# A fused attention and highway kernel: one query load in two pieces, the last stores in pairs, and a new order of work

## The chip, the cores and the metric

The kernel runs on one core of a Trainium2 chip. A core has five engines that work side by side, each with its own queue: TensorE (PE in the profile, with its weight loads as PEld), VectorE (DVE), ScalarE (ACT), GpSimd (POOL) and SyncE (SP), which computes nothing and issues transfers. Transfers (DMAs) that SyncE or ScalarE issue run on the core's DMA engines. The metric is the device time of one execution in microseconds (us), lower is better.

## What is computed

Eight batches of eight heads, 576 positions, 64 values each: an attention without the usual score matrix, then a highway layer on the 4608 x 512 result.

```python
def _attn_ref(q, k, v):
    q_s = softmax of q over its last axis
    k_s = softmax of k over the positions
    kv = np.einsum('bhsd,bhse->bhde', k_s, v)
    return np.einsum('bhsd,bhde->bhse', q_s, kv)

def _moe_ref(x, w_h, w_t, b_t):
    H = np.maximum(x @ w_h, 0.0)
    T = 1.0 / (1.0 + np.exp(-(x @ w_t + b_t)))
    return T * H + (1.0 - T) * x
```

The first function is shortened here: in the reference each softmax is written out. Between the two, x is the attention's output with the heads side by side, one row of 512 for each position.

## The kernel before

Each batch gives four and a half tiles of 128 rows; two batches share the ninth, so tile 8, 17, 26 and 35 hold rows of two batches, and 36 tiles come from four pairs of batches (`tiles`, from L129). A position is p * 9 + j, with p in 64 partitions for each of two heads and j from 0 to 8.

All work is a list of steps, `ORDER` (L16 to L64), and `tc.manual_schedule()` (L465) emits them in this order. Each engine executes its own steps in the order of the list; between engines the framework puts in the waits that the data and the buffers need. It also gives each DMA one of a few semaphores that tells of its landing. A suffix names an engine where there is a choice: A for ScalarE, D for VectorE, P for GpSimd.

For each batch b:

- `k_b_c`, `q_b_j`, `v_b_c` load (L187, L192), in SyncE's queue. `ld` has 3 buffers for each of k and v, `ldq` 4 for q. k and v of batches 0 and 1 come in two halves (c = 0 and 2). `Q_CUTS` (L176) is empty, so `q_b_0` is the whole query of a batch; `load_q` (L190) already knows a second piece.
- `ek` and `eq` (L244, L291): the exponentials on ScalarE. `vc` (L250) casts v, on GpSimd if no suffix says otherwise.
- `kv` (L263): 72 small matmuls, or 36 for one half; `kr` and `kn` (L275, L281) normalize into `kvb` on VectorE.
- `qt` and `qc` (L304, L313): eq transposed on TensorE, and the result moved out of PSUM.

For each tile i:

- `xu` (L331, TensorE), `rs` and `x` (L340, L346, VectorE): attention output, normalized, in 16 bits. Tiles 0 and 4 are done in two halves.
- `xt` (L353, TensorE) and `xe` (L360, ScalarE or VectorE): x transposed.
- `bw` (L372): the bias into a gate bank of PSUM, by a copy on ScalarE (`:A`) or a matmul. `mt` (L384) and `mh` (L393): four matmuls each for gate and carry.
- `th` (L406, L408): tanh on ScalarE. `dd` (L412) on VectorE. `uu` (L425): (tanh + 1) * d on VectorE. `oo` (L442): u + x on GpSimd.
- Where `uu_i_0` has the suffix P, the tile is called lifted: th goes to SBUF, and GpSimd does `ee` (d + x), `uu` (tanh * d) and `oo`. Before, tiles 4, 9, 22 and 26 are lifted.
- `st_i_h_r` (L451, L453, L455): the store. Neighbouring tiles share a buffer of `op` (7 buffers, tag o32) and are stored as a pair in two halves of the partitions, 256 KB each; the steps bear the number of the second tile. Tiles without a mate take a buffer of `o1p` (5 buffers) each. `mate` (L430) gives None for the ninth tiles and for i >= LAST - 4, so tiles 31 to 34 are stored singly, each in two DMAs of 128 KB (L453).
- Tile 35 is split in three by columns (`columns`, L144): 256, 128 and 128 wide, with a gate bank, `th`, `uu`, `oo` and `st` for each. Its first two stores are ScalarE's.

`fill_n_...` (L172): n matmuls of zeros, which keep TensorE at work where it has nothing else to do.

Of the kernel before, what the change touches and what calls it, by code (L numbers as in the profile page):

```python
# [16 lines left out]
b_0 b_32 setuppool fill_16_turned setupdve v_0_0 q_0_0 k_0_0 k_0_2 v_0_2 w_h_0 bsplit w_h_2 vc_0_1:A w_t_0 vc_0_0:D  # L17
fill_4_turned bp bc w_t_2 eq_0_0 v_1_2 eq_0_1 fill_14_xu_0_0 qt_0_0 k_1_2 qc_0_0 ek_0_1 ek_0_0 ek_0_2 k_1_0
fill_7_xu_0_0 kv_0_0 ek_0_3 kr_0_0 kn_0_0 vc_0_2:A vc_0_3 q_1_0 fill_5_xu_0_0 xu_0_0 eq_0_2 rs_0_0 fill_1_xu_0_1
kv_0_1 x_0_0 bw_0 whc_0 qt_0_1 kr_0_1 half qc_0_1:A kn_0_1 v_1_0 whd_1 fill_3_xu_0_1 xu_0_1 whc_2 bw_1 xu_1_0 xt_0_0  # L20
rs_0_1 whd_0 xe_0_0 rs_1_0 x_0_1 v_2_0 wtc_0 fill_2_mh_0_0 mh_0_0 x_1_0 xt_0_1 whd_3 fill_1_qt_1_0 xu_2_0 whd_2 mt_0_0
xe_0_1:D rs_2_0 wtc_2:D xt_1_0 mh_0_1 xe_1_0 x_2_0 mt_0_1 mt_1_0 dd_0 k_2_0 th_0_0 xt_2_0 uu_0_0 xu_3_0 th_1_0 mh_1_0
rs_3_0 xe_2_0 x_3_0 bw_2:A mh_2_0 dd_1 ek_1_3 mt_2_0 ek_1_2 vc_1_3 oo_0_0 vc_1_2 q_2_0 uu_1_0 dd_2 xt_3_0 bw_3 th_2_0
kv_1_1 xe_3_0:D ek_1_1 uu_2_0 mt_3_0 ek_1_0 kr_1_1 kn_1_1 mh_3_0 th_3_0 k_3_0 eq_1_0 dd_3 oo_1_0 oo_2_0 fill_4_qt_1_0
qt_1_0 uu_3_0 vc_1_0:A vc_1_1 bw_4 qc_1_0 eq_1_1 oo_3_0 fill_1_xu_4_0 kv_1_0 v_3_0 kr_1_0 fill_1_xu_4_0 qt_1_1 kn_1_0
qc_1_1:A fill_1_xu_4_0 xu_5_0 xu_4_0 rs_5_0 vc_2_2 rs_4_0 x_5_0 bw_5:A fill_2_xu_4_1 qt_0_2 eq_1_2 x_4_0 fill_1_xu_4_1
xt_5_0 qc_0_2:A xu_6_0 q_3_0 vc_2_0:A xu_4_1 qt_1_2 ek_2_2 k_4_0 v_4_0 q_4_0 xe_5_0:D rs_4_1 rs_6_0 mh_5_0 x_6_0
xt_4_0 qc_1_2 mt_5_0 x_4_1 xe_4_0:D dd_5 xt_4_1 xu_7_0 th_5_0 mt_4_0 xe_4_1:D rs_7_0 ek_2_0 xt_6_0 mh_4_0 mt_4_1
mh_4_1 k_5_0 uu_5_0 x_7_0 xe_6_0:D kv_2_0 dd_4 mh_6_0 kr_2_0 kn_2_0 xt_7_0 dd_6 xe_7_0:D oo_5_0 bw_7:A th_4_0 eq_2_0
uu_4_0:P bw_6:A eq_2_1 qt_2_0 ee_4 xu_8_0 mt_6_0 ek_3_0 rs_8_0 oo_4_0 x_8_0 mt_7_0 th_6_0 qc_2_0 ek_3_2 xt_8_0 uu_6_0  # L30
xu_9_0 mh_7_0 rs_9_0 oo_6_0 eq_2_2 x_9_0 xe_8_0 qt_2_1 dd_7 th_7_0 xu_10_0 xt_9_0 bw_8:A mh_8_0 rs_10_0 vc_3_2 uu_7_0
vc_3_0:A x_10_0 mt_8_0 oo_7_0 dd_8 xe_9_0 kv_3_0 qc_2_1 th_8_0 bw_9:A xt_10_0 uu_8_0 qt_2_2 mh_9_0 eq_3_0 kr_3_0
xe_10_0:D st_5_0_1 oo_8_0 kn_3_0 mt_9_0 bw_10:A v_5_0 eq_3_1 dd_9 xu_11_0 mh_10_0 rs_11_0 ee_9 th_9_0 x_11_0 mt_10_0
eq_3_2 qc_2_2 dd_10 bw_11:A xt_11_0 xu_12_0 th_10_0 uu_9_0:P xe_11_0:D qt_3_0 q_5_0 ek_4_0 rs_12_0 mh_11_0 oo_9_0
x_12_0 uu_10_0 qc_3_0:A xt_12_0 mt_11_0 xe_12_0:D oo_10_0 dd_11 bw_12:A xu_13_0 th_11_0 qt_3_1 rs_13_0 st_1_0_0 vc_4_2
mt_12_0 x_13_0 qc_3_1:A st_1_0_1 uu_11_0 xt_13_0 xu_14_0 ek_4_2 k_6_0 mh_12_0 oo_11_0 rs_14_0 xe_13_0:D x_14_0 mh_13_0
th_12_0 dd_12 bw_13:A xt_14_0 xu_15_0 vc_4_0 uu_12_0 xe_14_0 mt_13_0 eq_4_1 rs_15_0 v_6_0 x_15_0 mh_14_0 dd_13 th_13_0
kv_4_0 bw_14:A oo_12_0 uu_13_0 eq_4_2 qt_3_2 eq_4_0 xt_15_0 kr_4_0 mt_14_0 qc_3_2 kn_4_0 xe_15_0 st_3_0_1 bw_15 dd_14
xu_16_0 th_14_0 mt_15_0 st_3_0_0 rs_16_0 ek_5_2 x_16_0 qt_4_0 uu_14_0 xu_17_0 qc_4_0:A xt_16_0 mh_15_0 rs_17_0 q_6_0
x_17_0 th_15_0 qt_4_1 xe_16_0:D bw_16:A dd_15 xu_18_0 qc_4_1:A xt_17_0 mh_16_0 rs_18_0 xe_17_0:D x_18_0 ek_5_0 mh_17_0  # L40
uu_15_0 st_7_0_1 xu_19_0 eq_5_0 dd_16 st_5_0_0 mt_16_0 rs_19_0 q_7_0 x_19_0 eq_5_2 xt_18_0 qt_5_0 th_16_0 dd_17
bw_17:A oo_13_0 oo_14_0 vc_5_2 vc_5_0 kv_5_0 uu_16_0 qc_5_0:A mt_17_0 kr_5_0 xe_18_0:D bw_18:A kn_5_0 xt_19_0 mh_18_0
th_17_0 v_7_0 xe_19_0:D ek_6_2 uu_17_0 xu_20_0 mt_18_0 rs_20_0 dd_18 bw_19:A qt_5_2 x_20_0 mh_19_0 oo_15_0 oo_16_0
oo_17_0 th_18_0 eq_5_1 uu_18_0 xt_20_0 xu_21_0 st_7_0_0 mt_19_0 oo_18_0 rs_21_0 xe_20_0 bw_20:A th_19_0 vc_6_0 ek_6_0
qc_5_2 x_21_0 qt_5_1 dd_19 xu_22_0 xt_21_0 mh_20_0 rs_22_0 uu_19_0 x_22_0 mt_20_0 bw_21:A xe_21_0:D dd_20 xu_23_0
th_20_0 mh_21_0 rs_23_0 oo_19_0 vc_6_2 qc_5_1:A uu_20_0 xt_22_0 st_19_0_1 mt_21_0 x_23_0 xe_22_0 oo_20_0 k_7_0 dd_21
qt_4_2 st_14_0_0 xu_24_0 th_21_0 mh_22_0 rs_24_0 st_10_0_0 qc_4_2 bw_22:A uu_21_0 eq_6_0 xt_23_0 st_8_0_0 mt_22_0
x_24_0 oo_21_0 dd_22 bw_23:A kv_6_0 th_22_0 xe_23_0:D st_10_0_1 ee_22 eq_7_0 qt_6_0 kr_6_0 mh_23_0 kn_6_0 uu_22_0:P
eq_6_1 xt_24_0 qc_6_0 xu_25_0 mt_23_0 bw_24:A rs_25_0 x_25_0 eq_6_2 st_21_0_1 qt_7_0 xe_24_0 dd_23 xu_26_0 th_23_0
st_21_0_0 xt_25_0 vc_7_2:A mh_24_0 rs_26_0 st_17_0_0 uu_23_0 x_26_0 mt_24_0 xe_25_0 dd_24 bw_25:A xu_27_0 th_24_0  # L50
# [17 lines left out]
def kernel(  # L68
# [11 lines left out]
    B, H, S, D = q.shape  # L80
    DM = H * D
    P = 128
# [38 lines left out]
    T = {}  # L121
# [378 lines left out]
```

## Time and profile before

| | |
|---|---|
| time, median of 3 runs | 124.64 us (124.41 to 125.02) |
| profiled run | 124.86 us, span 122.9 us |
| granted TensorE clock, mean | 0.986 |
| read and written | 30.41 MB and 9.44 MB |

The span runs from the first to the last instruction of the profiled execution. Row 2 of the profile's page cuts it into 40 slices of 3.07 us; each digit is the busy share of a slice in tenths (9 is 90% or more), and the last row has the transfer rate.

```profile
PE   5999999999999999999999999999999999999200
DVE  5802899977989999989999999999999999998510
ACT  4279456887899999999999999899999687774200
POOL 5000102845328684988538547969739564464500
DMA  3999999999999999999999999999989305988842
```

The loads fill the DMA engines up to about 89 us; what follows is stores. A group of instructions in the profile is named by its line, engine and operands, `SPq` is SyncE's queue of DMA issues, and "<-" in a wait stands before what ended it.

### The profile page before, as it was taken

To read this page: it belongs to the slowest core of one execution; us is meant where nothing else is said; L and a number is where in the kernel's file an instruction comes from. 1 tells how busy PE (TensorE), PEld (TensorE's weight loads), DVE (VectorE), ACT (ScalarE), POOL (GpSimd) and SP (SyncE) were. 2 spreads that over 40 slices of the span, in tenths; PEclk is the share of its full clock that TensorE was granted. 3 is DMA by queue.
4 is the path that set the end of the run, shared out by engine and by line. 5 is a ranking of instruction groups with operands and counts; after the bars stand their busy time and mean duration, and the time that the engine had idled before them with its cause. 6 is when DMAs were issued, how large, how long until landed. Compare 5 with 4: busy or idle time off the path is not lost.

```text
span 122.9 us, 3478 instructions
## 1 busy us (share of the span) xinstructions
PE 112.5 (92%) x1392; PEld 65.7 (53%) x1392; DVE 100.9 (82%) x239; ACT 96.3 (78%) x150; POOL 63.9 (52%) x66
## 2 busy tenths in 40 slices
PE   5999999999999999999999999999999999999200
PEld 4645545445556665665566656566665655655100
DVE  5802899977989999989999999999999999998510
ACT  4279456887899999999999999899999687774200
POOL 5000102845328684988538547969739564464500
PEclk9999999999999999999999999999999999999995
DMA  3999999999999999999999999999989305988842
GB/s 119 382 403 402 412 387 391 392 395 381 389 392 388 392 389 388 392 386 402 392 401 396 395 400 403 393 400 395 402 275 249 76 0 108 237 277 264 203 113 87
DMA packets 17077, 40.08 MB, mean 326 GB/s; under 512 B 1187, under 2 KB 1571, under 8 KB 17061
## 3 DMA queue, kind: packets, MB, share of 16 engines
q1 hardware_dynamic: 16768, 39.65, 90.8%
q8 instruction: 11, 0.18, 0.6%
q10 hardware_dynamic: 292, 0.20, 0.5%
q14 instruction: 6, 0.04, 0.1%
HBM read 30.41 MB, written 9.44 MB: 324 GB/s over the span
## 4 chain that ended last, share of the span: by engine, by line
PE 61%; DMA 23%; SPq 3%; ACT 3%; POOL 2%; issue 2%; DVE 1%; DVEq 0%; POOLq 0%
PE tps L384 20%; PE gps L393 20%; DMA v<-in_v_dram 11%; DMA w32h<-in_moe_w_h_dram 8%; PE qps L304 6%; PE xu L331 6%; PE turned L353 6%; PE kv L263 4%; DMA out_dram<-o 3%; POOL o L442 2%; SPq L187 2%; SPq L453 1%; ACT eq L313 1%; ACT qe L291 1%; DVE u L425 1%
## 5 line engine op out<-in xcount | busy, mean ns | idle before, releaser
L442 POOL TENSOR_TENSOR o<-u,x 128x512 f32<-128x512 f16 (+1 forms) x32 | 36.2, 1132 | 30.4 <-DVE u L425 27.2
L384 PE MATMUL tps<-w16t,xT 128*128 128x512 f16 (+2 forms) x152 | 37.1, 368 | 0.0
L393 PE MATMUL gps<-w16h,xT 128*128 128x512 f16 x144 | 36.9, 379 | 0.1
L346 DVE TENSOR_TENSOR x<-xu,rs 128x512 f16<-128x512 f32 (+1 forms) x38 | 24.8, 657 | 0.5
L425 DVE SCALAR_TENSOR_TENSOR u<-tps,d 128x512 f16<-128x512 f32 (+2 forms) x34 | 22.3, 658 | 3.2 <-ACT tps L408 1.4
L412 DVE SCALAR_TENSOR_TENSOR d<-x,gps 128x512 f16<-128x512 f16 x36 | 24.2, 673 | 0.8 <-PE gps L393 0.7
L250 POOL CAST v<-v 128x1152 f16<-128x1152 f32 (+1 forms) x13 | 12.9, 996 | 19.5 <-DMA v<-in_v_dram 19.5
L408 ACT ACTIVATE tps<-tps 128x512 f32<-128x512 f32 (+2 forms) x34 | 18.8, 560 | 4.3 <-PE tps L384 4.0
L291 ACT ACTIVATE qe<-q 128x1024 f16<-128x1024 f32 (+1 forms) x24 | 19.7, 839 | 0.8 <-DMA q<-in_q_dram 0.8
L393 PEld LDWEIGHTS <-xT 128*128 128x128 f16 x144 | 12.8, 98 | 12.4 <-ACT xT L360 0.9
L384 PEld LDWEIGHTS <-xT 128*128 128x128 f16 x152 | 13.4, 98 | 11.2 <-issue 0.2
L244 ACT ACTIVATE ek<-k 128x1152 f16<-128x1152 f32 (+1 forms) x20 | 18.9, 968 | 0.5 <-DMA k<-in_k_dram 0.5
L374 ACT COPY tps<-ball 128x512 f32<-128x512 f32 (+1 forms) x31 | 18.0, 584 | 0.8 <-DVE u L425 0.8
L360 ACT COPY xT<-turned 128x512 f16<-128x512 f16 (+1 forms) x19 | 10.9, 574 | 4.7 <-PE turned L353 4.6
L331 PE MATMUL xu<-kvb,eq 128*128 128x130 f16 (+1 forms) x160 | 14.5, 224 | 0.1
L353 PE MATMUL turned<-idh,x 128*128 128x128 f16 x144 | 14.3, 220 | 0.0
L353 PEld LDWEIGHTS <-x 128*128 128x128 f16 x144 | 10.4, 98 | 6.9 <-DVE x L346 2.7
L304 PE MATMUL qps<-idh,qe 128*128 128x128 f16 x144 | 12.0, 219 | 0.2
L331 PEld LDWEIGHTS <-eq 128*128 128x128 f16 (+1 forms) x160 | 9.9, 100 | 3.7 <-DVE kvb L281 0.8
L304 PEld LDWEIGHTS <-qe 128*128 128x128 f16 x144 | 9.5, 98 | 4.1 <-ACT qe L291 0.8
L313 DVE COPY eq<-qps 128x1024 f16<-128x1024 f16 (+1 forms) x15 | 7.3, 488 | 4.1 <-PE qps L304 4.0
L313 ACT COPY eq<-qps 128x1024 f16<-128x1024 f16 (+1 forms) x9 | 8.5, 940 | 2.5 <-PE qps L304 2.5
(49 smaller groups left out, 98.9 us busy)
## 6 DMA issues: line engine op xcount, KB each, us to landing
q<-in_q_dram SPq DMA_DIRECT2D x8, 1152.0 KB, 13.7
out_dram<-o SPq DMA_DIRECT2D x31, 256.0 KB, 6.2
v<-in_v_dram SPq DMA_DIRECT2D x6, 1152.0 KB, 15.4
k<-in_k_dram SPq DMA_DIRECT2D x6, 1152.0 KB, 15.5
v<-in_v_dram SPq DMA_DIRECT2D x4, 576.0 KB, 10.8
k<-in_k_dram SPq DMA_DIRECT2D x4, 576.0 KB, 10.3
w32h<-in_moe_w_h_dram SPq DMA_DIRECT2D x2, 512.0 KB, 9.8
w32t<-in_moe_w_t_dram SPq DMA_DIRECT2D x2, 512.0 KB, 11.4
```

Source lines behind the costliest of these rows:

```text
L244: nc.scalar.activation(t[:, :, c:c + n].rearrange("p j c d -> p c j d"), T[f"k32{b}"][:, c:c + n].rearrange("p c (j d) -> p c j d", j=NJ), ...
L291: nc.scalar.activation(t[:, j0:j1].rearrange("p j c d -> p c j d"), T[f"q32{b}"].rearrange("p c (j d) -> p c j d", j=NJ)[:, :, j0:j1], AF.Exp)
L304: nc.tensor.matmul(t[:, (j - j0) % 2, 2 * kk:2 * kk + 2, (j - j0) // 2], T[f"qe{b}"][:, j, 2 * kk:2 * kk + 2].rearrange("p c d -> p (c d)" ...
L331: nc.tensor.matmul(dst, T[f"eq{b}_{jp // 2}"][:, jp % 2, n], kvb[b % NKV][:, hh, kk], start=True, stop=True, skip_group_check=True)
L346: nc.vector.tensor_mul(t[:, k0:k1], sums(i, k)[:, :, :, 0:64], T[f"rs{i}_{k}"][:, 0:k1 - k0].unsqueeze(3).to_broadcast([P, k1 - k0, 4, D]))
L353: nc.tensor.matmul(t[:, n], T[f"x{i}"][:, dims(n)], idh, is_transpose=True, start=True, stop=True, skip_group_check=True)
L384: nc.tensor.matmul(gate_bank(i, k if i == LAST else 0), T[f"xT{i}"][:, n], w16["t"][:, n, cs], start=False, stop=(n == 3), skip_group_chec ...
L393: nc.tensor.matmul(t, T[f"xT{i}"][:, n], w16["h"][:, n], start=(n == 0), stop=(n == 3), skip_group_check=True)
L408: nc.scalar.activation(src, src, AF.Tanh, scale=0.5)
L412: nc.vector.scalar_tensor_tensor(t, T[f"x{i}"], -0.5, T[f"gps{i}"], op0=ALU.mult, op1=ALU.max)
L425: nc.vector.scalar_tensor_tensor(t[:, 0:cs.stop - cs.start], gate_bank(i, h), 1.0, T[f"d{i}"][:, cs], op0=ALU.add, op1=ALU.mult)
L442: eng.tensor_add(t[:, 0:w], T[f"u{i}_{h}"][:, 0:w], T[f"{'e' if lifted(i) else 'x'}{i}"][:, cs])
```

## The change

Three edits of the code, and a new list.

```diff
-    Q_CUTS = {}
+    Q_CUTS = {1: 4}
...
     def mate(i):
-        return None if i % 9 == 8 or i >= LAST - 4 else i + 1 if i % 9 % 2 == 0 else i - 1
+        return None if i % 9 == 8 else i + 1 if i % 9 % 2 == 0 else i - 1
...
         if mate(i) is not None:
             eng.dma_start(dst[:, 2 * (jp + r) - 2:2 * (jp + r)], T[f"oo{i - 1}"][rows])
-        elif len(bs) == 1:
-            eng.dma_start(dst[:, 4 * (jp // 2) + 2 * r + jp % 2], T[f"o{i}_{h}"][rows])
         else:
```

The query of batch 1 comes in two pieces, `q_1_0` with positions j = 0 to 3 and `q_1_4` with the rest. Tiles 31 and 32, and 33 and 34, become pairs: `st_31` and `st_33` are gone, `st_32` and `st_34` store both tiles, and their outputs lie in `op` instead of `o1p`.

The list is written anew; it has 706 steps instead of 707. Its beginning up to the second batch's first tiles, before:

```
b_0 b_32 setuppool fill_16_turned setupdve v_0_0 q_0_0 k_0_0 k_0_2 v_0_2 w_h_0 bsplit w_h_2 vc_0_1:A w_t_0 vc_0_0:D
fill_4_turned bp bc w_t_2 eq_0_0 v_1_2 eq_0_1 fill_14_xu_0_0 qt_0_0 k_1_2 qc_0_0 ek_0_1 ek_0_0 ek_0_2 k_1_0
fill_7_xu_0_0 kv_0_0 ek_0_3 kr_0_0 kn_0_0 vc_0_2:A vc_0_3 q_1_0 fill_5_xu_0_0 xu_0_0 eq_0_2 rs_0_0 fill_1_xu_0_1
...
kv_1_1 xe_3_0:D ek_1_1 uu_2_0 mt_3_0 ek_1_0 kr_1_1 kn_1_1 mh_3_0 th_3_0 k_3_0 eq_1_0 dd_3 oo_1_0 oo_2_0 fill_4_qt_1_0
qt_1_0 uu_3_0 vc_1_0:A vc_1_1 bw_4 qc_1_0 eq_1_1 oo_3_0 fill_1_xu_4_0 kv_1_0 v_3_0 kr_1_0 fill_1_xu_4_0 qt_1_1 kn_1_0
qc_1_1:A fill_1_xu_4_0 xu_5_0 xu_4_0 rs_5_0 vc_2_2 rs_4_0 x_5_0 bw_5:A fill_2_xu_4_1 qt_0_2 eq_1_2 x_4_0 fill_1_xu_4_1
xt_5_0 qc_0_2:A xu_6_0 q_3_0 vc_2_0:A xu_4_1 qt_1_2 ek_2_2 k_4_0 v_4_0 q_4_0 xe_5_0:D rs_4_1 rs_6_0 mh_5_0 x_6_0
```

and after:

```
b_0 b_32 setuppool fill_16_turned setupdve v_0_2 k_0_2 q_0_0 k_0_0 v_0_0 w_h_0 bsplit w_h_2 vc_0_3 w_t_0 fill_4_turned
bp ek_0_2 w_t_2 vc_0_2:A ek_0_3 v_1_2 bc fill_8_xu_0_1 kv_0_1 kr_0_1 kn_0_1 eq_0_0 k_1_2 fill_10_xu_0_1 qt_0_0 k_1_0
qc_0_0 fill_4_xu_0_1 xu_0_1 rs_0_1 half vc_0_1 vc_0_0:D q_1_0 x_0_1 whc_0 v_1_0 q_1_4 k_2_0 v_2_0 q_2_0 bw_1:A ek_0_1
eq_0_1 eq_0_2 ek_0_0 bw_0:A fill_6_xu_0_0 kv_0_0 qt_0_1 kr_0_0 xt_0_1 whd_0 kn_0_0 xe_0_1 qc_0_1:A whc_2 fill_3_xu_0_0
xu_0_0 xu_1_0 rs_0_0 rs_1_0 x_0_0 x_1_0 wtc_0 fill_3_mh_0_0 xt_0_0 xe_0_0:D fill_2_mh_0_0 xt_1_0 whd_1 xu_2_0 whd_2
xe_1_0 mh_0_0 whd_3 wtc_2:D mt_0_0 mh_0_1 rs_2_0 x_2_0 mt_0_1 mh_1_0 dd_0 th_0_0 vc_1_2:A xt_2_0 uu_0_0 xu_3_0 xe_2_0
mt_1_0 dd_1 ek_1_2 rs_3_0 bw_2 vc_1_3 oo_0_0 mt_2_0 th_1_0 x_3_0 ek_1_3 uu_1_0 mh_2_0 ek_1_0 oo_1_0 ek_1_1 xt_3_0
kv_1_1 xe_3_0:D th_2_0 dd_2 mh_3_0 eq_1_0 uu_2_0 fill_1_qt_1_0 qt_1_0 kr_1_1 vc_1_0:A vc_1_1 k_3_0 kn_1_1 bw_3:A
oo_2_0 fill_1_xu_4_1 kv_1_0 dd_3 qc_1_0:A mt_3_0 kr_1_0 ee_3 kn_1_0 eq_1_1 xu_4_1 xu_5_0 rs_5_0 th_3_0 rs_4_1
fill_1_bw_5 qt_1_1 v_3_0 x_5_0 eq_1_2 uu_3_0:P bw_4:A bw_5 qc_1_1 xt_5_0 xu_4_0 fill_1_xu_6_0 xu_6_0 oo_3_0 qt_0_2
ek_2_2 q_3_0 vc_2_0 k_4_0 v_4_0 q_4_0 xe_5_0:D rs_4_0 x_4_1 mt_5_0 rs_6_0 x_4_0 x_6_0 xt_4_0 mh_5_0 th_5_0 xe_4_0:D
```

Its end, before:

```
x_35_0 oo_30_0 st_30_0_1 oo_31_0 st_26_0_0 st_25_0_1 st_30_0_0 st_31_0_1 st_31_0_0 th_33_0 xt_35_0 uu_33_0 mt_34_0
xe_35_0:D bw_35_0:A dd_34 mh_35_0 th_34_0 oo_32_0 st_32_0_0 oo_33_0 st_32_0_1 st_25_0_0 mt_35_0 uu_34_0 st_33_0_1
bw_35_1 mt_35_1 dd_35 bw_35_2 oo_34_0 mt_35_2 st_33_0_0 th_35_1 th_35_0 th_35_2 st_34_0_0 st_34_0_1 uu_35_1 uu_35_0
oo_35_1 uu_35_2 st_35_1_0:A oo_35_0 oo_35_2:P st_35_0_0:A st_35_2_0
```

and after:

```
uu_31_0 xu_34_0 xe_33_0 mt_32_0 rs_34_0 dd_32 bw_33:A mh_33_0 x_34_0 oo_29_0 oo_30_0 st_30_0_1 st_26_0_0 th_32_0
st_8_0_0 xt_34_0 uu_32_0 st_30_0_0 xu_35_0 xe_34_0:D mt_33_0 bw_34:A rs_35_0 dd_33 mh_34_0 x_35_0 th_33_0 mt_34_0
uu_33_0 dd_34 xt_35_0 bw_35_1 th_34_0 bw_35_2 bw_35_0 oo_31_0 oo_32_0 st_32_0_1 oo_33_0 st_32_0_0 xe_35_0:D st_23_0_0
uu_34_0 mh_35_0 oo_34_0 mt_35_0 dd_35 mt_35_1 mt_35_2 th_35_1 th_35_0 st_34_0_0 th_35_2 st_34_0_1 uu_35_1 uu_35_0
oo_35_1:P uu_35_2 oo_35_0 oo_35_2:P st_35_1_0:A st_35_0_0:A st_35_2_0
```

Between the two, the lifted tiles are now 3, 4, 9, 10, 12, 14, 16 and 27; some of the copies and casts (`vc`, `qc`, `xe`, `bw`) go to another engine; and in SyncE's queue the loads from batch 5 on stand ahead of stores that they followed before:

```
before: k_5_0 st_5_0_1 v_5_0 q_5_0 st_1_0_0 st_1_0_1 k_6_0 v_6_0 st_3_0_1 st_3_0_0 q_6_0 st_7_0_1 st_5_0_0 q_7_0 v_7_0 ...
after:  k_5_0 q_5_0 v_5_0 k_6_0 st_1_0_1 st_1_0_0 v_6_0 st_3_0_0 st_5_0_1 st_3_0_1 st_5_0_0 q_6_0 st_7_0_0 q_7_0 ...
```

## What was predicted

> **What bounds the kernel now.** I read the busy times first, then the busy time by stretch, then the chain of work that ended last, then the waits of the engines and of SyncE's queue, and last the timeline of the tail.
>
> ```profile
> PE 112.5 (92%) x1392; PEld 65.7 (53%) x1392; DVE 100.9 (82%) x239; ACT 96.3 (78%) x150; POOL 63.9 (52%) x66
> ...
> 25.00:30.00 5.00, 4.88 (x70) 2.60 (x68) 3.56 (x10) 3.91 (x7) 2.92 (x3) 1.00 1.05 386
> 60.00:70.00 10.00, 10.00 (x159) 6.28 (x157) 9.73 (x23) 9.98 (x14) 5.87 (x6) 1.00 1.05 396
> 115.00:122.90 7.90, 0.00 (x0) 0.00 (x0) 0.97 (x4) 0.00 (x0) 0.46 (x2) 0.77 0.50 126
> ```
>
> The columns of a stretch are its length, then PE, PEld, DVE, ACT, POOL, clock, DMA share and GB/s. In the middle PE is full, with DVE and ACT close behind; in the last 7.9 us it does nothing. At 25 to 30 it looks full, but part of that is filler (L172). The chain shows both ends:
>
> ```profile
> 13.38 14.12 DMA v<-in_v_dram
> 27.50 0.02 issue
> 27.53 0.67 ACT v L250
> 28.20 0.97 ACT qe L291
> ...
> 104.88 0.88 PE tps L384 x4
> ...
> 115.38 1.91 DMA out_dram<-o
> 117.29 0.03 issue
> 117.32 0.02 DVEq L442
> 117.34 0.04 issue
> 117.38 0.42 DVE o L442
> ```
>
> I went through PE's start times with 216 ns for each 512-wide matmul (0.86 us for four): from 32.32, where mh_5 starts, to 114.11 all gaps together are 1.45 us. That stretch is **PE's**. Before it PE has eleven fillers after the first mh (11 x 0.216 = 2.4 us) and 1.9 us of gaps, waiting for batch 1. After it comes a tail of 8.7 us.
>
> The timeline of SyncE's queue in the tail:
>
> ```profile
> 114.24 4.81 SPq L453 DMA_DIRECT2D out_dram<-o  x4
> 117.31 0.47 SPq L453 DMA_DIRECT2D out_dram<-o  x1
> 120.21 0.34 SPq L455 DMA_DIRECT2D out_dram<-o  x1
> ```
>
> The waits, in us, times and the longest:
>
> ```profile
> SPq L453 <- DMA out_dram<-o: 2.5, 1, 2.5
> SPq L455 <- DMA out_dram<-o: 1.1, 1, 1.1
> DVE o L442 <- DMA out_dram<-o: 1.8, 1, 1.8
> POOL o L442 <- DVE u L425: 27.2, 25, 4.3
> ```
>
> SyncE issues st_33_0_1 at 114.24 and then stands 2.5 us before st_33_0_0. The DMA records name each transfer's semaphore: st_33_0_0 has the same one as ScalarE's st_35_1_0, issued at 115.38 and landed at 117.29. So the queue's head waits for a store that comes later in the list. oo_35_0 on DVE waits for that same landing, and st_35_2_0 (120.21) waits for ScalarE's st_35_0_0 in the same way. st_34, whose data POOL had ready at 115.03, goes out at 117.87 and 118.46.
>
> **What the skill says.** The page TensorE: Matmul & The Clock Gate (section "Wait — 56ns, not 53.3ns?") gives 215.7 ns from start to start of warm 512-wide matmuls; the trace agrees (0.86 for four). The page Perfetto Trace Analysis ("DMA Instruction — HWDGE (DVE, Sync)") says that the reported bar is the issue alone and that the semaphore comes only after the write is confirmed; here bars of 0.34 to 0.60 us land 1.5 to 5.1 us after their start. The page DMA: Bandwidth & Descriptors ("Issuing engines are not separate DMA queues") says that queues of different engines share the DMA engines, so another issuer saves only issue time; the 0.38 us of a ScalarE issue fits. GPSIMD Engine Reference ("4.1 Engine selection") has two-input operations about twice as slow on POOL; here 1.155 against 0.69 us.
>
> **The change, tail.** Take 109.42, where PE starts mt_33, as zero; both lists have xu_35 before it and mh_34 after it. Before: xt_35 at 1.73, mt_34 to 2.82, mh_35 to 3.69, mt_35 and its two bias matmuls to 4.69; oo_34 4.46 to 5.61; last landing 12.34 (121.76); end 13.43. After, with those durations: mt_34 moves ahead of xt_35, so PE has mt_33, mh_34, mt_34 to 2.59, xt_35 to 2.81, three bias matmuls to 3.03 (0.11 more than before; bw_35_0 leaves ACT, whose 0.38 there was hidden). Then PE waits for xe_35 on DVE: 0.17 to the result, 0.41 to copy, so mh_35 starts at 3.5 and mt_35 ends at 5.23. **PE ends 0.54 later.** In return th_34 runs 2.76 to 3.35, uu_34 after xe_35 to 4.15, oo_34 4.2 to 5.35. Pairing 31/32 and 33/34 turns eight 128 KB stores into four of 256 KB: SyncE's last ones are st_32 (twice, after oo_32 at about 2.4), st_23_0_0, st_34 (twice), st_35_2. Four issues of about 0.57 us leave the queue, st_23_0_0 (0.6 to 1.0) enters it ahead of st_34, in time that SyncE would spend waiting for oo_34. With nothing to wait for, st_34 goes out at 5.45 and 6.0 instead of 8.45 and 9.04. A 256 KB store landed 2.96 us after its start on an idle queue (the one at 101.74) and 4.2 behind others: last st_34 lands at 9.0 to 10.2. The three parts of tile 35: uu_35 at 5.65 to 6.5 (0.42 after PE's end, as before), oo_35_1 on POOL 6.0 to 6.4 (0.42), oo_35_2 to 7.0, oo_35_0 on DVE to 6.9 with all three buffers taken before the stores. ScalarE stores at 6.5 and 6.95, landing at 9.3 (2.31 as before); st_35_2 at 7.05, landing at 8.6 to 9.7. I take 9.7 for the last landing, plus the 1.09 that the end took: 10.8. **Tail: 13.4 - 10.8 = 2.6 saved**, 2.1 to 3.0 by the landings.
>
> **Head.** Stores and loads share SyncE's ring, so a landing follows from the bytes ahead. Before: k_1_0 22.99, q_1 26.00, v_1_0 27.50. After: 4/9 of q_1 (0.52 MB at 0.39 MB/us) 24.3, v_1_0 25.85, the rest 27.5. The two pieces have rows of 1024 and 1280 B; packets of 1024 B took 46 ns in the trace and of 2304 B 95, so the pieces cost some 0.1 us more of 3.1. The additional issue (0.37 to 0.5) lies where SyncE stands[...] (bars of 2.2 to 2.8). The chain through eq_1_1 can start at 27.6 instead of 28.11, and qc_1_1 moves from ACT (1.01, after a wait of 0.7) to DVE (0.68): eq_1_1 to 28.65, qt_1_1 to 29.3, qc_1_1 to 30.0, xu_6 at 30.1 against about 31.7. ACT may refuse part of this: th_0, vc_1_2, xe_2, four ek, th_1, th_2, eq_1_0, vc_1_0, bw_3, qc_1_0 stand before eq_1_1, 8 us at its measured pitch from a start of 19.3 to 20.2, which gives 27.3 to 28.2. The list's fillers after the first mh fall from 11 to 4, 1.5 us. Against it, batch 0 begins with v_0_2 and k_0_2, q_0 lands at 9.1 instead of 7.6, and kv_0_0 waits until about 13.4; DVE's weight casts then bring mh_0_0 at 17.5 to 18.2 instead of 16.79, with xu_2 and xt_1 already behind it. I take **1.2 saved**, bounds 0 and 1.8. More is impossible: q_2 still lands near 36.5, and qt_2_0 needs eq_2_0 at 37.6. k_2 ahead of v_2 is free: ek_2_2 has its data at 30.5, and v_2 at 33.5 plus a cast of 1.15 is before kv_2_0.
>
> **Middle.** Lifted tiles go from 4 to 8. DVE: 4 x 0.69 less u, three xe more (1.24), one eviction less (0.68), oo_35_1 less: -2.5. ACT: two casts (2.31), one eviction (1.01) and about 0.8 of bias copies more, three xe less (1.75): +2.4. POOL: 4 x 2.31 less 2 x 1.14, plus 0.42: +7.4, to 71. All stay under PE. Bias matmuls on PE in mid-list: bw_15 goes, bw_7 comes, nothing. Loads from batch 5 on go ahead of stores, which takes nothing from PE, since no wait of an engine for a load is seen after 34; a store held longer (pair 22/23) leaves at most two pairs alive at 31/32 of seven buffers. I put 0 here, with -0.3 to +0.5.
>
> **Sum.** 2.6 + 1.2 = 3.8: 122.9 - 3.8 = 119.1 for the span. The profiled run took 124.86 (124.41 to 125.02 in the others, median 124.64), so the time is 124.64 - 3.8 = **120.8**.
>
> **Rivals.** Half a per cent, 0.62 us, is what can be told from no change here.
> A, as forecast: 120.8, 119.4 to 122.2; chance 0.62.
> B, the head gives nothing, since ACT before eq_1_1 or batch 2's landing sets the pace: 124.64 - 2.6 = 122.0; 0.14. For it: ACT's idle time at 20 to 30 is small (4.33 of 5 us busy at 20 to 25). Against: the fillers.
> C, the change doesn't do what it says: st_34 or st_35_2 still shares a semaphore with a ScalarE store, which the diff doesn't show, since nothing in the code names semaphores. Then the tail gives 0 and 124.64 - 1.2 = 123.4; 0.12. Against: four stores fewer stand between.
> D, both fail: 124.6; 0.04.
> E, slower: **POOL becomes the bound** between tiles 9 and 18. It is busy 21.2 of 30 us in 50 to 80; tiles 10, 12, 14 and 16 add 9.2 there, two casts leave (2.3), so 28.1 of 30. If it can't fill its idle time, because a lifted tile's three operations (3.46) stand ahead of the next o, then d and u (three buffers each) run out and dd waits on DVE, and PE behind it. It decides once PE waits over 4.4 us; at 5 us 125.8; 0.08. For it: POOL's waits for u are spread over 25 places. Against: those waits vanish for tiles whose u POOL makes.
>
> **Chances.** Faster A + B + C = 0.88, same D 0.04, slower E 0.08. From 119.4 to 123.2 lie A, B and part of C.
>
> **What would show it.** After: SyncE issues st_34 within 0.2 us of oo_34, and no wait of SPq or DVE for out_dram is over 0.5 us after PE's end; PE's end to the end of the span is about 5.6 us; one PE gap of 0.4 to 0.6 before mh_35; four fillers after the first mh, and PE full from about 31. Wrong if POOL is busy over 95% in 50 to 80 with DVE's dd waiting for it, or if ACT's eq_1_1 starts after 28.2.

## The result, and the profile after

| | before | changed kernel |
|---|---|---|
| time, median | 124.91 us (124.41 to 125.17, 6 runs) | 123.50 us (123.41 to 123.89, 6 runs) |
| ratio | | 0.990, 95% interval 0.9876 to 0.9924 |
| profiled span | 122.9 us | 121.4 us |

The change makes the kernel faster by about 1.3 us (1.0%), where 3.8 us were forecast: the direction is right, and the size is outside the range. The same kernel, measured again later beside other runs (c0_after_again), had 0.9915 (0.9889 to 0.9941). A few executions of four kernels below took over 1.5% more than the fastest of the same kernel; the times and ratios leave them out.

The busy times of the changed kernel:

```profile
PE 110.7 (91%) x1388; PEld 65.1 (54%) x1388; DVE 98.7 (81%) x236; ACT 97.1 (80%) x151; POOL 71.4 (59%) x73
```

POOL has 7.5 us more (forecast 7.4), DVE 2.2 less (forecast 2.5), ACT 0.8 more (forecast 2.4). The same stretches as before, in the same columns:

```profile
25.00:30.00 5.00, 4.82 (x103) 2.69 (x101) 3.71 (x10) 5.00 (x8) 3.88 (x4) 1.00 1.06 384
60.00:70.00 10.00, 9.77 (x156) 6.19 (x155) 9.62 (x22) 10.00 (x16) 7.95 (x9) 1.00 1.05 398
115.00:121.40 6.40, 0.00 (x0) 0.00 (x0) 1.25 (x4) 0.52 (x3) 0.96 (x2) 0.67 0.53 132
```

Between 60 and 70 us PE is no longer quite full. PE ends 0.7 us later than before, and from its end to the end of the span it takes 6.6 us instead of 8.7 (5.6 were forecast). SyncE's queue in the tail:

```profile
108.21 7.90 SPq L451 DMA_DIRECT2D out_dram<-o  x6
116.72 0.34 SPq L453 DMA_DIRECT2D out_dram<-o  x1
```

and its waits from 112 us to the end:

```profile
SPq L493 <- DMA out_dram<-o: 3.2, 1, 3.2
SPq L451 <- POOL o L442: 1.6, 1, 1.6
SPq L453 <- POOL o L442: 0.5, 1, 0.5
```

No store waits for the landing of another any more. The only wait for a landing is that of the kernel's last line (L493), for everything. The wait of SyncE for POOL is that of st_34 for oo_34: oo_34 ends at 114.97, and st_34 goes out at 115.00 and 115.51, as forecast (5.45 and 6.0 after the start of mt_33; measured 5.43 and 5.94). PE's gap ahead of mh_35 is there too, about 0.5 us: the last of the three bias matmuls starts at 112.51 and takes 0.11, and mh_35 starts at 113.08:

```profile
112.40 0.38 PE L376 MATMUL tps<-b,ones 128*128 128x128 f16 x3
113.08 1.04 PE L393 MATMUL gps<-w16h,xT 128*128 128x512 f16 x4 [0.30 <-DVE xT L360]
```

From mt_33's start (109.57) to the end the tail takes 11.8 us; before it took 13.4. So 1.6 of the forecast 2.6 us came. And mt_33 itself starts 0.15 us later than before, so of the 1.2 us forecast for the head nothing is left there. In the head, this is how the chain of waits begins in this profile:

```profile
4.08 12.52 DMA w32h<-in_moe_w_h_dram
16.61 0.02 issue
16.63 0.69 DVE w16h L218
17.32 0.03 issue
17.36 0.28 DVE rs L340 x2
17.63 0.77 DVE x L346 x2
```

whc_2 (L218) stands on VectorE in front of rs_0_0 to x_1_0 and waits for the second half of w_h. That half lands at 16.61; before, whc_2 began at 15.64. PE's timeline shows what this does:

```profile
18.05 0.28 PE L353 MATMUL turned<-idh,x 128*128 128x128 f16 x2 [1.04 <-DVE x L346]
...
19.30 0.59 PE L393 MATMUL gps<-w16h,xT 128*128 128x512 f16 x2
```

The first carry matmul starts at 19.30 instead of 16.79. Part of this is chance: in the second profile of the same kernel (c0_after_again) that half has landed by 15.33, whc_2 starts at 16.02 without a wait, PE's gap is 0.24 instead of 1.04 us, and the first carry matmul starts at 18.70. After it there are four fillers, as forecast, but at 32 us PE is hardly ahead: mt_5 starts at 32.0, and by the work that stands before it in the list the same point was reached at about 32.2 before.

### The profile page after: what moved, and what is told of

Read it like the earlier page. It is cut to its first block, busy times and chain, and to the rows that moved or that the text cites. A ratio compares the mean times of both kernels' runs of the same rounds, so it can differ in the third digit from the quotient of the medians.

```text
span 121.4 us, 3467 instructions
## 1 busy us (share of the span) xinstructions
PE 110.7 (91%) x1388; PEld 65.1 (54%) x1388; DVE 98.7 (81%) x236; ACT 97.1 (80%) x151; POOL 71.4 (59%) x73
## 4 chain that ended last, share of the span: by engine, by line
PE 68%; DMA 10%; DVE 7%; ACT 3%; SPq 3%; issue 2%; POOL 1%; POOLq 0%; DVEq 0%
PE tps L384 23%; PE gps L393 22%; DMA w32h<-in_moe_w_h_dram 10%; PE xu L331 7%; PE turned L353 6%; PE qps L304 5%; PE kv L263 3%; DVE u L425 2%; SPq L187 2%; POOL o L442 1%; DVE x L346 1%; DVE xT L360 1%; ACT tps L408 1%; DVE d L412 1%; ACT eq L313 1%
## 5 line engine op out<-in xcount | busy, mean ns | idle before, releaser
L442 POOL TENSOR_TENSOR o<-u,x 128x512 f32<-128x512 f16 (+1 forms) x29 | 32.1, 1108 | 23.2 <-DVE u L425 19.3
L346 DVE TENSOR_TENSOR x<-xu,rs 128x512 f16<-128x512 f32 (+1 forms) x38 | 24.8, 656 | 0.6
L250 POOL CAST v<-v 128x1152 f16<-128x1152 f32 (+1 forms) x11 | 11.0, 1000 | 19.7 <-DMA v<-in_v_dram 18.4
L408 ACT ACTIVATE tps<-tps 128x512 f32<-128x512 f32 (+2 forms) x30 | 16.6, 559 | 6.8 <-PE tps L384 6.8
L425 DVE SCALAR_TENSOR_TENSOR u<-tps,d 128x512 f16<-128x512 f32 (+2 forms) x30 | 19.4, 652 | 2.6 <-ACT tps L408 1.8
L374 ACT COPY tps<-ball 128x512 f32<-128x512 f32 x32 | 19.0, 596 | 0.8 <-DVE u L425 0.8
L360 ACT COPY xT<-turned 128x512 f16<-128x512 f16 (+1 forms) x16 | 9.0, 562 | 3.5 <-PE turned L353 3.4
L360 DVE COPY xT<-turned 128x512 f16<-128x512 f16 (+1 forms) x22 | 8.9, 406 | 2.2 <-PE turned L353 1.6
L423 POOL TENSOR_TENSOR u<-th,d 128x512 f16<-128x512 f16 x8 | 9.2, 1154 | 0.7 <-ACT th L406 0.7
```

The lines of the kernel that those rows point to most:

```text
L346: nc.vector.tensor_mul(t[:, k0:k1], sums(i, k)[:, :, :, 0:64], T[f"rs{i}_{k}"][:, 0:k1 - k0].unsqueeze(3).to_broadcast([P, k1 - k0, 4, D]))
L360: copy(t[:, 2 * k0:2 * k1], T[f"xtps{i}"][:, 2 * k0:2 * k1])
L425: nc.vector.scalar_tensor_tensor(t[:, 0:cs.stop - cs.start], gate_bank(i, h), 1.0, T[f"d{i}"][:, cs], op0=ALU.add, op1=ALU.mult)
L442: eng.tensor_add(t[:, 0:w], T[f"u{i}_{h}"][:, 0:w], T[f"{'e' if lifted(i) else 'x'}{i}"][:, cs])
```

## The experiments

The verdict of every run is its ratio to the kernel before, measured beside it, with its 95% interval; us is the median:

| run | edit | us | ratio (95%) |
|---|---|---|---|
| e1_tail_alone | before + pairs and buffers at the end | 122.98 | 0.9829 (0.9791 to 0.9866) |
| e7_buffers_alone | before + buffers taken first | 124.92 | 0.9978 (0.9961 to 0.9996) |
| g1_sync_only | e7 + no store on ScalarE at the end | 122.72 | 0.9819 (0.9783 to 0.9856) |
| h3_pairs_sync | e1 + no store on ScalarE at the end | 122.76 | 0.9827 (0.9800 to 0.9854) |
| e2_single_33 | changed kernel, 33 and 34 single | 124.00 | 0.9908 (0.9878 to 0.9939) |
| h1_no_st34 | changed kernel without st_34 | 121.28 | 0.9713 (0.9681 to 0.9744) |
| i1_early_pairs | h3 + six stores earlier | 122.55 | 0.9814 (0.9787 to 0.9842) |
| i2_single_late | h3 + 33 and 34 single | 122.08 | 0.9771 (0.9744 to 0.9797) |
| h2_stores_early | h3 + both | 121.86 | 0.9751 (0.9726 to 0.9776) |
| e6_cut_alone | before + query in two pieces | 125.21 | 1.0005 (0.9986 to 1.0023) |
| e4_query_whole | changed kernel, query whole | 124.17 | 0.9926 (0.9898 to 0.9954) |
| e3_whc2_late | changed kernel, whc_2 later | 123.93 | 0.9908 (0.9876 to 0.9941) |
| h4_first_loads | changed kernel, first loads reordered | 125.66 | 1.0081 (1.0041 to 1.0121) |
| f1_xt35_first | changed kernel, xt_35 ahead of mt_34 | 123.49 | 0.9871 (0.9838 to 0.9905) |
| f3_new_middle | f1 with before's head | 122.99 | 0.9835 (0.9800 to 0.9869) |
| f2_new_head | e1 with the new head | 124.18 | 0.9942 (0.9921 to 0.9963) |
| e5_four_lifted | changed kernel, four tiles not lifted | 126.91 | 1.0147 (1.0109 to 1.0186) |
| c0_after_again | changed kernel once more | 123.87 | 0.9915 (0.9889 to 0.9941) |

### The tail alone

The list of before, with the code's pairs and a new end:

```diff
- st_31_0_1 st_31_0_0 ... st_33_0_1 ... st_33_0_0
- uu_35_1 uu_35_0 oo_35_1 uu_35_2 st_35_1_0:A oo_35_0 oo_35_2:P st_35_0_0:A st_35_2_0
+ uu_35_1 uu_35_0 oo_35_1:P uu_35_2 oo_35_0 oo_35_2:P st_35_1_0:A st_35_0_0:A st_35_2_0
```

> The kernel before with the change's tail alone: tiles 31/32 and 33/34 stored in pairs (st_31 and st_33 gone), the three outputs of tile 35 computed before its first store, oo_35_1 on GpSimd. Head, middle and the order of xt_35 and mt_34 are those of before. Theory 1 (the wait of SyncE and VectorE for ScalarE's store is what the tail cost, and the stores then land in one burst): PE ends at about 114.1 as before, st_34 is issued within 0.2 us of oo_34 at about 115.1 and 115.7, the last landing is near 120.3 instead of 121.8, so 1.4 to 1.8 us less than before, about as much as the whole change (1.4). Rival (the change's gain came from its head or its middle): no more than 0.5 us less than before.

Measured: 0.9829, that is 2.1 us. The tail alone gains more than the whole change. Everything else in the new list together therefore costs about 0.9 us. SyncE's waits from 112 us on hold the wait that the forecast's rival C is about:

```profile
SPq L455 <- DMA out_dram<-o: 2.4, 1, 2.4
SPq L451 <- POOL o L442: 2.4, 1, 2.4
```

The last store of all, st_35_2, still waits 2.4 us for a landing: the DMA records give it the semaphore of ScalarE's st_35_1_0 (issued at 115.40, landed at 118.56). Only st_34 is free of such a wait: it goes out at 115.01 and 115.52. So the shared semaphore is still there, at another place in the queue, and the gain came all the same.

### Which part of the tail: the buffers, the semaphore or the pairs

First the buffers of tile 35 alone, in the list of before:

```diff
- st_35_1_0:A oo_35_0 oo_35_2:P st_35_0_0:A st_35_2_0
+ oo_35_0 oo_35_2:P st_35_1_0:A st_35_0_0:A st_35_2_0
```

> The kernel before with one step moved: oo_35_0 and oo_35_2 stand ahead of st_35_1_0, so the three outputs of tile 35 don't take the buffer that st_35_1_0 is still reading. All stores are those of before. Theory 1 (two separate faults, the buffer and the shared semaphore): VectorE no longer waits 1.8 us, st_35_0_0 is issued near 116.1, but SyncE still stands before st_33_0_0 until a store of ScalarE has landed at about 117.3, st_34_0_1 lands near 121.0, so 0.6 to 0.9 us less than before. Rival (the buffer is the one cause, and the semaphore's wait goes with it): 1.5 to 2 us less than before.

Measured: 0.9978. SyncE's waits in this run, from 112 us on, hold the two of before (2.5 and 1.1 us) unchanged:

```profile
SPq L453 <- DMA out_dram<-o: 2.5, 1, 2.5
SPq L495 <- DMA out_dram<-o: 1.2, 1, 1.2
SPq L455 <- DMA out_dram<-o: 1.1, 1, 1.1
```

Then the same kernel with all stores of tile 35 on SyncE; tiles 31 to 34 are still single, so the number of stores is that of before:

```diff
- oo_35_0 oo_35_2:P st_35_1_0:A st_35_0_0:A st_35_2_0
+ oo_35_0 oo_35_2:P st_35_1_0 st_35_0_0 st_35_2_0
```

> The kernel before, with the three buffers of tile 35 taken before its stores (as in e7_buffers_alone, 0.998), and all three stores of tile 35 on SyncE in place of two on ScalarE; tiles 31 to 34 are stored singly as before. Theory 1, the shared semaphore is the cost, the number of stores is not: with one queue a semaphore can only wait for a store issued earlier, SyncE has no wait for a landing after 114, st_33_0_0 goes out at about 115, the last landing comes at about 120.3 instead of 122.2, and the ratio is 0.985 to 0.988. Theory 2, the gain of the pairs comes from four issues fewer: SyncE is busy issuing to 118, the last landing stays above 121.5, and the ratio is 0.995 to 0.998.

Measured: 0.9819. SyncE's waits from 112 us on in this run:

```profile
SPq L495 <- DMA out_dram<-o: 1.2, 1, 1.2
SPq L495 <- PEq L495: 0.6, 2, 0.4
SPq L453 <- POOL o L442: 0.5, 1, 0.5
```

The waits of L453 and L455 for a landing are gone, st_33_0_0 goes out at 114.88 right behind st_33_0_1 (114.29), and the last landing is at 119.62 instead of 122.15. Two suffixes in the list, which give SyncE two issues more to do, win 2.0 us over e7_buffers_alone (0.9819 against 0.9978). So the number of SyncE's issues is not what cost. What the suffixes take away is the two waits, and ScalarE's stores with them; that the latter don't cost by themselves is shown next. The Trainium skill's page DMA: Bandwidth & Descriptors, section "Why a DMA increments its semaphore by 16 and not by 1", says that two transfers in flight on one semaphore can't be told apart by its count; that is a reason for a framework to hold the second one back. No run here shows such a count; what the traces show is the wait, 2.5 us at the head of SyncE's queue.

The counterpart is the pairs, with nothing on ScalarE. It differs from e1_tail_alone by the same two suffixes:

> e1_tail_alone with the two stores of ScalarE given to SyncE; beside g1_sync_only (0.982) it differs in the pairs 31/32 and 33/34 alone. Theory 1, the pairs add nothing once the semaphore is not shared: 0.980 to 0.984. Theory 2, pairs save issues of SyncE and bring the last issue forward by 0.5 us: 0.977 to 0.979. If pairs hold bytes of tile 33 back until 34 is done and so cost: 0.985.

Measured: 0.9827. With nothing on ScalarE, pairs and singles are equal (0.9827 against 0.9819). And e1_tail_alone, with two stores on ScalarE and a wait of 2.4 us for one of them, is as fast (0.9829). So neither ScalarE's stores nor a wait for a landing cost by themselves: in e1 only st_35_2, 64 KB, stands behind the wait, before the change st_33_0_0 and both halves of st_34 did. The pairs won because with them no such wait stands in front of st_34 any more; nothing else in them shows in the time.

The changed kernel with 33 and 34 single again shows the same from the other side:

```diff
-         return None if i % 9 == 8 else i + 1 if i % 9 % 2 == 0 else i - 1
+         return None if i % 9 == 8 or i >= LAST - 2 else i + 1 if i % 9 % 2 == 0 else i - 1
...
- oo_33_0 st_32_0_0 xe_35_0:D st_23_0_0
+ oo_33_0 st_32_0_0 xe_35_0:D st_23_0_0 st_33_0_1 st_33_0_0
```

> The changed kernel with tiles 33 and 34 not paired: st_33 goes out in two 128 KB halves right after oo_33 and st_34 in two after oo_34, all by SyncE. Theory 1 (after PE's end the last stores are limited by what the DMA engines move: 768 KB issued from 115.0 on land by 120.3): 256 KB fewer are left at the end, at some 0.25 to 0.3 MB per us that is 0.6 to 1.0 us earlier, so about 122.6 to 122.9 against 123.5 of the changed kernel. Rival (the fixed time from a store's issue to its landing sets the end, or the two additional stores bring a semaphore that is still in use): within 0.3 us of the changed kernel, or slower by 1 us or more, with a wait of SyncE for out_dram in the tail.

Measured: 0.9908, no gain over the changed kernel. With two more stores the semaphores come round once more, as SyncE's waits from 112 us on show:

```profile
SPq L453 <- DMA out_dram<-o: 2.2, 1, 2.2
SPq L495 <- DMA out_dram<-o: 1.4, 1, 1.4
```

The DMA records name the pair: the second half of st_34 goes out at 118.20 on the semaphore of ScalarE's store of 116.47, which landed at 118.19. So this run didn't test what it was made for.

### Why the last stores landed late

The forecast took 2.31 us from issue to landing for ScalarE's second store (128 KB), from before; it took 3.79 (116.46 to 120.25). The first one (64 KB) took 3.88, and 1.91 before. The next run leaves out the two DMAs st_34, so the rows of tiles 33 and 34 are not written:

```diff
- th_35_0 st_34_0_0 th_35_2 st_34_0_1 uu_35_1
+ th_35_0 th_35_2 uu_35_1
```

> The changed kernel without the two DMAs st_34, so the rows of tiles 33 and 34 are not written: 0.5 MB less in the last burst. Theory 1, the last stores land late because their bytes stand behind st_34's: ScalarE's stores land 2.3 us after their issue as in before (3.9 in the changed kernel), the last landing is about 118.7 instead of 120.45, and the ratio 0.976 (the changed kernel 0.990). Theory 2, the latency of 3.9 us belongs to the stores themselves, whatever is ahead: the last landing moves by under 0.4 us, ratio 0.987 or more.

Measured: 0.9713, and ScalarE's two stores land 1.59 and 1.79 us after their issue. In the changed kernel the same stores therefore take 2.0 to 2.3 us more because of st_34's bytes. In the stretch from 117 to 119 us (the last two columns are DMA share and GB/s) the changed kernel has

```profile
117.00:119.00 2.00, 0.00 (x0) 0.00 (x0) 0.00 (x0) 0.00 (x0) 0.00 (x0) 0.54 0.97 244
```

and the kernel without st_34

```profile
117.00:119.00 2.00, 0.00 (x0) 0.00 (x0) 0.00 (x0) 0.00 (x0) 0.00 (x0) 1.00 0.34 104
```

The DMA engines are busy 97% of the time at 244 GB/s. What had not gone out when tile 34 was done, 0.52 MB of st_34 and 0.26 MB of tile 35, takes 0.79 / 0.244 = 3.2 us at that rate, in whatever order. The packets themselves run from 116.12 to 119.97, that is 3.85 us and 204 GB/s on the average; the first moves 1.1 us after st_34's issue, and the last landing comes 0.5 us after the last packet. The older stores have all landed by 115.75.

If that is right, tile 33 should leave on its own, before tile 34 is done, and older stores that have landed by then don't matter. Two edits of h3_pairs_sync make one each, and a third makes both:

```diff
 older stores (i1, h2):
- st_19_0_0 ... st_16_0_1 ... st_23_0_0 ... st_26_0_0 st_25_0_1 ... st_25_0_0
+ oo_25_0 st_19_0_0 st_16_0_1 st_23_0_0 st_25_0_1 st_25_0_0 ... oo_26_0 st_26_0_0
 single 33 and 34 (i2, h2), with the mate() of e2_single_33:
- oo_33_0 st_32_0_1
+ oo_33_0 st_32_0_1 st_33_0_1 st_33_0_0
```

> e1_tail_alone (0.983) with three more edits at the end: all stores of tile 35 on SyncE; tiles 33 and 34 single again, so that 33 leaves before 34 is done; and six older stores (st_19_0_0, st_16_0_1, st_23_0_0, st_25 twice, st_26_0_0) moved into the time from 94 to 101 in which SyncE stands idle. Theory 1, the end is set by the bytes that are left when tile 34 is done: SyncE has no backlog at 113, the last landing is at 118.8, ratio 0.975. Theory 2, only the shared semaphore mattered: 0.981 to 0.983, as g1_sync_only.

> h3_pairs_sync (0.983) with the six older stores moved into SyncE's idle time at 94 to 101, and 33/34 still a pair, so h2_stores_early (0.975) less the single stores. Theory 1, what counts are the bytes that can only leave after tile 34 is done (0.75 MB with the pair, 0.5 MB with single stores): the older stores change nothing, since theirs have landed by 115.7 in any case, and the ratio stays at 0.981 to 0.983. Theory 2, the backlog of older stores is what holds the last ones back: 0.975 to 0.977.

> h3_pairs_sync with tiles 33 and 34 single and the older stores where they were, st_25_0_0 behind st_33. Theory 1, the bytes left after tile 34: tile 33 leaves at 113 and the last landing comes 1 us earlier, ratio 0.975 to 0.977. Theory 2, the backlog: st_33 and st_25_0_0 stand behind older stores, nothing is won, 0.981 to 0.983, as g1_sync_only.

Measured: both 0.9751, older stores alone 0.9814, single stores alone 0.9771. The older stores are worth 0.2 to 0.3 us, which isn't told apart from nothing; the single stores 0.7 us over h3_pairs_sync. SyncE's queue in h2_stores_early:

```profile
110.62 1.83 SPq L451 DMA_DIRECT2D out_dram<-o  x2
113.04 3.05 SPq L453 DMA_DIRECT2D out_dram<-o  x4
116.19 1.51 SPq L457 DMA_DIRECT2D out_dram<-o  x3
```

st_33 goes out at 113.04, st_34 at 114.99, and the last landing is at 118.91. h2_stores_early beats both kernels: 121.86 us. A rival is the form of the packets: a half of a pair moves rows of 4096 B and a single store rows of 2048 B. The traces speak against it. From 90 us on, most packets of 4096 B in the changed kernel took about 159 or 310 to 340 ns, and most packets of 2048 B in h2_stores_early about 84 or 150 to 175, so for a byte the two forms take the same; and in h2_stores_early, the fastest run, the packets of 2048 B from 116 to 118 us took 165 ns (median), which is the slow kind.

### The head

The query's cut alone, in the list of before:

```diff
-    Q_CUTS = {}
+    Q_CUTS = {1: 4}
...
- v_1_0
+ v_1_0 q_1_4
```

> The kernel before with the cut of the query alone: q_1_0 holds positions 0 to 3, v_1_0 follows, then q_1_4. Nothing else is moved. Theory of the forecast (v_1_0's landing at 27.5 sets when batch 1 can start): vc_1_0 stands before eq_1_1 on ScalarE and kv_1_0 comes earlier, eq_1_1 starts at 27.6 to 27.8 instead of 28.1, 0.3 to 0.5 us less. Rival (ScalarE's and PE's order in the list sets it, with fillers already placed): less than 0.2 us either way, or slower by the additional SyncE issue and the shorter rows (0.1 to 0.3 us).

Measured: 1.0005, nothing. And the changed kernel without the cut (`Q_CUTS = {}`, no q_1_4):

> The changed kernel with the query of batch 1 whole again, ahead of v_1_0. Theory of the forecast: v_1_0 lands 1.6 us later (28.1 instead of 26.6), vc_1_0 and with it bw_3, qc_1_0 and eq_1_1 on ScalarE are 1 us later, 0.7 to 1.2 us more than the changed kernel. Rival (there is slack before batch 2): less than 0.3 us more.

Measured: 0.9926, not to be told apart from the changed kernel (0.990 and 0.9915). The cut does what it should: eq_1_1 starts at 30.36 without it and at 28.46 with it (c0_after_again). But this is worth nothing that can be measured in either list.

The wait of whc_2, moved behind whd_1:

```diff
- qc_0_1:A whc_2 fill_3_xu_0_0 ... whd_1 xu_2_0 whd_2
+ qc_0_1:A fill_3_xu_0_0 ... whd_1 xu_2_0 whc_2 whd_2
```

> The changed kernel with one step moved: the cast of the second half of w_h (whc_2) stands behind whd_1 on VectorE instead of ahead of rs_0_0, rs_1_0, x_0_0 and x_1_0. Theory 2 (in the changed kernel's head VectorE's in-order queue waits for w_h's landing, and tile 0 and 1 behind it): x_0_0 about 0.8 us earlier, the gap of PE of 1.2 us before xt_0_0 mostly gone, 0.3 to 0.8 us less than the changed kernel. Rival (batch 1's and batch 2's loads or ScalarE set the pace of the head, so that time won before them is waited out later): within 0.2 us of the changed kernel.

Measured: 0.9908, no change. The first carry matmul starts at 18.54 instead of 18.70 to 19.30, and nothing of it is left at the end. The run says little of the wait itself: in its own profile that half of w_h has landed by 15.31, so there was hardly a wait to take away.

The order of the first five loads:

```diff
- v_0_2 k_0_2 q_0_0 k_0_0 v_0_0
+ v_0_2 q_0_0 k_0_2 k_0_0 v_0_0
```

> The changed kernel with its first five loads in the mirrored order of before: v_0_2, q_0_0, k_0_2, k_0_0, v_0_0 instead of v_0_2, k_0_2, q_0_0, k_0_0, v_0_0. Theory 1, two half loads in front are what makes the new order start slowly: all five have landed by 12.1 instead of 12.6, every later load comes 0.5 us earlier, and the ratio is 0.986. Theory 2, the slow start belongs to something else, and k_0_2, now 1.5 us later, delays the first kv: landings unchanged within 0.2, ratio 0.990 to 0.993.

Measured: 1.0081, worse than either theory said. The single executions lie between 125.19 and 127.04, so the size is not sure. The five loads have landed by 12.32 instead of 12.58, where the kernel before had 12.09, so the order explains about half of the 0.5 us. The first load of all goes with the rest: v_0_2 lands at 4.8 to 5.3 us in all ten profiles that begin with it, v_0_0 at 4.3 to 4.5 in the ten that begin with that; why isn't shown. But k_0_2 lands at 9.32 instead of 6.52, the first carry matmul starts at 21.09, 1.8 to 2.4 us later than in the two profiles of the changed kernel, and PE ends at 116.7, 1.9 to 2.1 us later. Nearly all of this delay is carried to the end.

To put a price on the head as a whole, the list was taken apart at mh_4_1, up to which both lists hold the same work but for two query copies and two transposes. First the changed kernel with before's order at the end:

```diff
- th_33_0 mt_34_0 uu_33_0 dd_34 xt_35_0 bw_35_1 th_34_0 bw_35_2 bw_35_0 ... xe_35_0:D ... mh_35_0
+ th_33_0 xt_35_0 uu_33_0 mt_34_0 xe_35_0:D bw_35_0:A dd_34 mh_35_0 th_34_0 ... bw_35_1 ... bw_35_2
```

> The changed kernel with xt_35 and xe_35 put back ahead of mt_34's successor, as before had them (th_33, xt_35, uu_33, mt_34, xe_35, bw_35_0 on ScalarE, dd_34, mh_35). Theory 1, the swap costs what the trace shows as a gap of 0.51 us ahead of mh_35: the gap is gone, PE ends 0.5 us earlier, and the time is 0.986 of before (the changed kernel 0.990). Theory 2, the end is set by how fast the last 0.75 MB of stores land and not by PE: PE ends earlier, but the last landing moves by less than 0.2 us, and the ratio stays at 0.989 to 0.991.

Measured: 0.9871, between the two theories. The gap ahead of mh_35 is gone. The intervals overlap with the changed kernel's, so up to 0.4 us may be won here, or nothing.

Then f1 with before's head, up to mh_4_1, in place of the new one (query whole, tile 3 not lifted):

> Before's head to mh_4_1 with the query whole and tile 3 not lifted, then the changed kernel's middle, with the end of f1_xt35_first. It differs from f1_xt35_first in the head and from e1_tail_alone mainly in the middle. Theory 1, the new middle loses about 0.5 us in PE gaps around tiles 17 and 24, where PE waits for VectorE and ScalarE: 0.987. Theory 2, the middle costs nothing, as forecast: 0.983, as e1_tail_alone.

Measured: 0.9835, as e1_tail_alone. The new middle costs nothing, and the new head costs 123.49 - 122.99 = 0.5 us where 1.2 us of gain were forecast; the two intervals overlap a little, so what is sure is that the head gains nothing. The busy time by stretch shows how, first f1 (new head)

```profile
16.00:32.00 16.00, 15.45 (x181) 8.44 (x180) 13.85 (x37) 12.89 (x21) 7.71 (x8) 1.00 1.06 383
32.00:95.00 63.00, 61.89 (x911) 37.55 (x909) 57.74 (x128) 61.40 (x91) 46.66 (x42) 1.00 1.04 385
```

and then f3 (head of before):

```profile
16.00:32.00 16.00, 15.77 (x184) 8.38 (x182) 13.85 (x36) 12.43 (x22) 7.69 (x8) 1.00 1.05 388
32.00:95.00 63.00, 62.70 (x918) 37.85 (x916) 58.94 (x133) 61.75 (x91) 45.20 (x40) 1.00 1.02 383
```

From 16 to 32 us the fillers' bars take 2.99 us of PE's time with the new head and 4.12 with the old one, so the new head does 15.45 - 2.99 = 12.5 us of useful matmuls there, the old one 11.7. It is ahead. From 32 to 95 us it loses 62.70 - 61.89 = 0.8 us in small gaps that f3 doesn't have, the longest at 36.9, 82.9 and 88.9 us.

The last 494 steps of the two lists are the same, so the same step can be looked up in both. VectorE's x (L346) starts 0.93 us earlier in f1 at 34.9 us, but only 0.03 to 0.04 earlier from 44.5 to 79.0, and then later: 0.33 us at 82.0, 0.71 at 90.7, 0.66 from 99.6 to the end. The places where this turns, in f1 (new head)

```profile
37.69 1.06 ACT L291 ACTIVATE qe<-q 128x1024 f16<-128x1024 f32 x1 [0.33 <-DMA q<-in_q_dram]
80.89 0.43 DVE L360 COPY xT<-turned 128x512 f16<-128x512 f16 x1 [0.45 <-ACT tps L408]
```

and in f3 (head of before):

```profile
37.69 1.07 ACT L291 ACTIVATE qe<-q 128x1024 f16<-128x1024 f32 x1
80.56 0.42 DVE L360 COPY xT<-turned 128x512 f16<-128x512 f16 x1
```

The first is eq_2_0. With the new head it waits for the query of batch 2, which lands at 37.66 (f3: 36.39), so the lead ends there; in c0_after_again it waits 0.34 us in the same way. The second is a copy of x, for which VectorE stands idle for 0.45 us until a tanh of ScalarE has ended; the two profiles of the changed kernel have the same wait, at 80.75 and 80.48, and f3 has not. Why the same step waits with one head and not with the other is not shown.

The last of these runs is the new head before e1's middle and end:

> The changed kernel's list to the end of mh_4_1 (with the query in two pieces and tile 3 lifted), then the rest of the list of e1_tail_alone, that is before's middle and before's order at the end with the pairs. It differs from e1_tail_alone (0.983) in the head alone. Theory 1, the new head gains 0.2 us of the forecast 1.2 and the new middle takes it back: 0.981. Theory 2, the new head itself loses, since w_h_2 lands later and the first carry matmuls start 2 us later: 0.985 or more, and the PE gap of 1.2 us at 17 to 18 is seen with no gain behind it. If the head gives what was forecast: 0.973.

Measured: 0.9942, worse than expected by 0.9 points. PE loses 1.45 us at one place:

```profile
36.31 0.27 PE L304 MATMUL qps<-idh,qe 128*128 128x128 f16 x2 [0.28 <-ACT eq L313]
38.26 0.77 PE L263 MATMUL kv<-v,ek 64*64 64x65 f16 x72 [1.45 <-DVE x L346]
```

kv_2 waits for an x on VectorE, which stands behind a query copy; this waited for TensorE's transposes, and these for ScalarE's query copy, which stands behind a cast of v. These two copies are among the steps that the cut of the lists moved, so this run says less of the head than f1 against f3: part of its loss is made by the splice.

### The middle

Four of the lifted tiles (10, 12, 14, 16) given back to VectorE:

```diff
- uu_10_0:P ... uu_12_0:P ... uu_14_0:P ... uu_16_0:P
+ uu_10_0 ... uu_12_0 ... uu_14_0 ... uu_16_0
```

> The changed kernel with tiles 10, 12, 14 and 16 not lifted: their u is VectorE's again, GpSimd has eight operations (9.2 us) less. Theory 3 (GpSimd, busy 94 to 99 per cent at 52 to 70 us, is not what PE's gaps in the middle come from; VectorE is nearly full): 0.5 to 2 us more than the changed kernel, with PE gaps of that sum between 45 and 75. Rival (the lifted tiles hold up d and u, and with them PE): up to 0.6 us less, and the PE gaps at 68 to 69 us vanish.

Measured: 1.0147, 3.0 us more than the changed kernel beside it. From 50 to 80 us PE is busy 27.5 instead of 29.8 of 30 us, and its waits name the chain (GpSimd was busy 15.6 us in this run and 26.6 in the changed kernel):

```profile
ACT tps L374 <- DVE u L425: 3.2, 3, 1.6
...
PE tps L384 <- ACT tps L374: 1.7, 2, 1.2
```

In this list the lifting is needed: it takes off VectorE what the list puts there.

The changed kernel itself, once more:

> The changed kernel unaltered, as a control beside the next three and for a second profile. If the late landing of the second half of w_h (the wait of VectorE's cast for it until 16.6) is the change's own, it is seen again within 0.3 us; if it was chance, w_h lands near 14.7 to 15.1 and mh_0_0 starts about 1 us earlier than 19.3.

Measured: 0.9915 and a span of 121.5 us. The second half of w_h lands at 15.33 instead of 16.61, so its late landing was chance for the most part. The first carry matmul starts at 18.70 instead of 19.30, and PE's last matmul starts at 114.7 (114.8 in the first profile), so the profile of one run says little about half a microsecond in the head.

## Why the prediction was right and wrong

**The cause in the tail was right.** The step "the queue's head waits for a store that comes later in the list" is shown by g1_sync_only and e7_buffers_alone: with the wait 0.998, without it 0.982. That the change takes this wait away was right too, and with it the direction. But it matters what stands behind the wait: e1_tail_alone has one of 2.4 us in front of the last 64 KB, as rival C has it, and loses nothing by it. Rival C (a semaphore still shared) didn't happen in the changed kernel, though its time, 123.4, is nearly the measured one; that is coincidence, since two other terms fell short. One more pair of stores brings the shared semaphore back (e2_single_33).

**Fewer issues were no part of it.** The forecast names "four issues of about 0.57 us leave the queue" among what the pairs bring. h3_pairs_sync against g1_sync_only shows that this is worth nothing.

**The tail's size was wrong, in one term.** Issues came within 0.1 us of the forecast. The step that failed is "ScalarE stores at 6.5 and 6.95, landing at 9.3 (2.31 as before); st_35_2 at 7.05, landing at 8.6 to 9.7": ScalarE's second store took 3.79 us, and st_35_2, the last landing of all, came at 10.9 in place of 9.7. That is the missing 1.0 us of 2.6. The 2.31 us of before were measured on a store that had 128 KB issued in the 0.6 us ahead of it; in the changed kernel 0.59 MB were issued in the 1.5 us ahead, and h1_no_st34 shows that these bytes are what it waits for. The stretches of before had a number for it: 126 GB/s at a DMA share of 0.50 after 115 us, which is some 250 GB/s at a full share. The forecast did not divide the bytes by it. That would have given 3.1 us for the 0.79 MB, and with 1.55 us from issue to landing, as st_35_2 of before took, a last landing at 10.1 (an estimate): nearer, but still short, since the bytes moved at 204 GB/s on the average. A small misreading goes with it: the bars of stores that the forecast gives as 0.34 to 0.60 us include one of 1.03, which is the one that took 5.1 us; the others in the tail took at most 4.6.

**The head's 1.2 us did not come.** The step that failed is "the chain through eq_1_1 can start at 27.6", that is, that batch 1 waits for v_1_0. v_1_0 landed at 26.56, but eq_1_1 started at 29.07, later than the 28.11 of before. The reserve that the forecast kept, "ACT may refuse part of this", is what happened: ScalarE works without a gap from th_0 at 21.23 to eq_1_1, the 8 us that the forecast counted, but from a start of 21.23 instead of 19.3 to 20.2, because "mh_0_0 at 17.5 to 18.2" became 19.3. In c0_after_again it is 18.7 for mh_0_0 and 28.46 for eq_1_1, still over the 28.2 that was to show the forecast wrong. And an earlier eq_1_1 would not have helped: "q_2 still lands near 36.5" became 37.34, since the new order starts its loads slowly (the first five have landed by 12.58 instead of 12.09, and k_3 lands at 40.35 instead of 39.48), and at eq_2_0 the lead of the new head ends. The cut is not the cause of the later loads; in e4_query_whole k_3 lands at 40.35 too. The fillers fell as forecast, but fewer fillers were taken for time won. Rival B, "the head gives nothing", is what happened, with the causes that it named, ScalarE ahead of eq_1_1 and the landing of batch 2; it had 0.14.

**The middle was right** in sum: f3_new_middle and e1_tail_alone are equal (0.9835, 0.9829). Rival E (POOL becomes the bound) didn't happen: POOL is busy 26.6 of 30 us at 50 to 80, where the forecast had 28.1. In the first half of that stretch it is nearly full, 14.77 of 15 us, and PE is full beside it. e5_four_lifted points the other way: without the lifting VectorE is too slow.

**The sum.** The tail with the order of before 2.1 us, the new head -0.5, the middle 0, the new order of mt_34 and xt_35 between -0.4 and 0: 1.2 to 1.6, against 1.1 to 1.4 measured. The head's -0.5 and the last term are near what these runs can tell from nothing. Two things are not settled: why the copy at 80.9 us waits for ScalarE with the new head alone, and what the late landing of q_2 costs by itself, since no run changed the loads' arrival alone and left the rest as it was.

## What to carry to other kernels

Where two engines issue transfers near the end, look at which semaphore each transfer has. A store that waits for the landing of another engine's later store holds up everything behind it in its queue: here that cost 2.0 us with 0.4 MB behind it, and nothing with the last 64 KB. Giving the stores to one queue can be all that is needed. Price the last stores by the bytes that can't leave earlier, divided by the rate that the tail shows, and add the time of a store that goes out alone; the landing time of one store that had little ahead of it is too short. A filler that disappears is not time won unless what follows it has its data earlier, and a lead in the head is lost at the first load that lands later than before.

## What the runs showed of the hardware that was not expected

- In the changed kernel's tail, stores alone kept the DMA engines busy 97% of the time at 244 GB/s (117 to 119 us), while with loads in the mix the same engines moved 384 to 398 GB/s. This is no fixed rate of stores: from 113.5 to 114 us they moved 360 GB/s at a share of 0.93.
- The packets of a store come in two speeds: 4096 B in about 159 or 310 to 340 ns (changed kernel), 2048 B in about 84 or 150 to 175 (h2_stores_early). What decides between them isn't shown.
- The same 128 KB store from ScalarE landed 1.79 us after its issue without st_34 (h1_no_st34), 2.31 in the kernel before, and 3.79 behind the 0.5 MB of st_34.
- At the start a late load is carried to the end: k_0_2 2.8 us later made PE end 1.9 us later (h4_first_loads), over 100 us after it. A load that only comes earlier did not show at the end: in e6_cut_alone v_1_0 lands at 26.02 instead of 27.50, and the time is the same.
